# Eight read buffers instead of four, and a new order of the last part, in a fused convolution and feed-forward kernel

## The chip, the cores and the metric

The kernel runs on one core of one Trainium2 chip. The metric is the device time of one execution in microseconds (us). Three timed runs of the kernel before took 190.89, 190.52 and 190.52 us, a median of 190.52.

The engines are named as the profile names them: PE (TensorE, matmuls; PEld its weight loads), DVE (VectorE), ACT (ScalarE), POOL (GpSimd) and SP (SyncE, which here only issues DMAs).

## The reference

The input `x` is [2048, 512] in bfloat16. Two branches work on its normalised rows:

```python
xn = layernorm(x)
kv = causal_conv4(k, shift_k) * v
y  = irfft(rfft(pad(kv)) * rfft(pad(ssm_k)))[:2048] + kv * ssm_D
s  = xn * y
h  = gelu(xn @ w_gate) * (xn @ w_up)      # 512 -> 1792
g  = silu(h @ w_down)                     # 1792 -> 512
return x + s * g
```

So one branch is a long convolution along the 2048 tokens, done through Fourier spectra, and the other is a gated feed-forward block. They meet in the last line.

## The kernel before

Tokens are held 16 to a partition: tile t (0 to 15) is token 16p + t on partition p, 512 channels wide. The transforms are matrix products in two stages, with a trip through DRAM between them (ZH, ZK, ZI), since the second stage needs the data across partitions. The last of these trips is ZI: the inverse transform's first stage (L1027, `inverse`) is copied out of PSUM into the buffers BO, stored to ZI from ACT's DMA queue, and read back into the buffers BI from SP's queue, when all 16 stores have landed. The read number j brings what the pair of tiles 2j and 2j+1 needs.

The feed-forward block works on four groups q of four tiles: 14 units m of gate and up projection (L641), gelu on ACT (L1193), product on DVE into HT (L1202), then the down projection of the group. For groups 0 to 2 the result is made silu by a tanh on ACT (L1234) and one DVE operation (L1236). Group 3 uses ACT's silu itself (L1242), which needs a table load on ACT first.

The last part of the program, from about 150 us on, has these pieces. The short names are used from here on:

- **y0 to y7** (PE, L1277): the second inverse stage of pair j, four matmuls with 64 columns of weights each, two side by side. It reads one BI buffer and fills two PSUM banks.
- **c0 to c7** (ACT or DVE, L1293, recorded in the helper's lines L632, L634, L635): copy of y's PSUM to a BO buffer, 128x1024. For pairs 6 and 7 the copy multiplies by 2.
- **x4, x5** (DVE, L1286): G times XN for pairs 4 and 5; x0 to x3 are done earlier.
- **p0 to p7** (DVE, L1294): product of the copy with G (pairs 0 to 5) or with XN (pairs 6 and 7).
- **a0 to a5** (DVE, L1306): plus X, and **o0 to o5** (SP): the output DMA of the pair, 256 KB.
- **D8 to D11**, **D12 to D15** (PE; L641 for the former, L1223 for the latter): down projection of a tile, in three parts a, b, c of 4, 5 and 5 steps. L1223 does each step in two halves of 64 columns side by side. D15 is 384 columns wide, and its remaining 128 columns, **D15'**, are 14 plain matmuls (L641).
- **s12 to s15, s15'** (ACT, L1242): silu; **m12 to m15'** (DVE, L1244): times the pair's product p6 or p7; **n12 to n15'** (DVE, L1245): plus X; **w12 to w15'** (SP): the output DMA, 128 KB (96 and 32 KB for tile 15).
- **HT0** and so on: the DVE product (L1202) of unit m of group 3.

The order on every engine is written out by hand: `SEQ` (L27 to L50) lists all 816 tasks by number. `Sched.run` (L348) walks that list, gives each task its engine (a trailing `b` takes the second choice, DVE instead of ACT for a copy), takes a free buffer from its pool where it needs one, and the tasks are emitted in that order. Each engine thus works through its own queue in the order of the list; a waiting instruction holds up all behind it on its engine, DMA issues too. Waits are derived from the overlaps of addresses and from use of the same PSUM bank (`Trk._need`, L137). The buffer that a task takes decides which earlier reader it waits for.

The buffers of the last part share room with older ones. HSW (eight slots of four 512-wide rows, 4 KB per partition each) holds the spectra: HS in slots 0 to 3, HW in slots 4 to 7. BI lies at the same address:

```python
HSW = new("HSW", [128, 8, 4, DM], BF16)                  # at kk_at + 2048
BI = at("BI", [128, 4, 4, DM], BF16, kk_at + 2048)
pBI = Pool_("BI", 4)
d_bi = [dsem(f"d_bi{j}") for j in range(4)]
```

Eight reads go through four buffers, so the fifth read takes the buffer of the first and waits until y of that pair has read it. PE is assigned the y tasks in any order that SEQ gives; the reads are issued in an order of their own.

Of the kernel before, what the change touches and what calls it, by code (L numbers as in the profile page):

```python
# [6 lines left out]
BF16 = mybir.dt.bfloat16  # L7
# [7 lines left out]
DM = 512  # L15
# [34 lines left out]
)  # L50
NF_BANKS = 4
ISSUE = 470.0
# [29 lines left out]
class Trk:  # L82
# [29 lines left out]
    def res(self, name, ap):  # L112
        t = ap.tensor
        tn = type(t).__name__
        if tn.startswith("SB"):
            key = "SB"
            addr = self.nc.lookup_mloc(t).addr
        else:
            assert tn.startswith("PS")
            key = "PS:" + t.name  # L120
            addr = 0
        esz = mybir.dt.size(ap.dtype)
        pairs = [list(q) for q in ap.ap]
        pst, pn = pairs[0]
        pstart = ap.offset // pst if pst else 0
        inner = ap.offset - pstart * pst
        hi = sum(st * (n - 1) for st, n in pairs[1:])
        r = Res(name, key, pstart, pstart + pn, addr + inner * esz, addr + (inner + hi + 1) * esz)
        lst = self.res_by_key.setdefault(key, [])
        for o in lst:  # L130
            if o.plo < r.phi and r.plo < o.phi and o.blo < r.bhi and r.blo < o.bhi:
                o.ovl.append(r)
                r.ovl.append(o)
        lst.append(r)
        return r
# [278 lines left out]
def build_kernel(nc, A_q, A_k, A_v, A_shift_k, A_ssm_k, A_ssm_D, B_w_gate, B_w_up, B_w_down, out):  # L414
    with ExitStack() as es0:
# [8 lines left out]
        def at(name, shape, dt, offset):  # L424
            return nc.alloc_sbuf_tensor_at(name, shape, dt, offset=offset)
# [40 lines left out]
        kk_at = place["at"]  # L466
# [27 lines left out]
        BK.append(at("BK2", [128, 4, DM], BF16, skb_at))  # L494
        assert place["at"] <= top, (place["at"], top)
        BO = at("BO", [128, 4, 2, DM], BF16, ast_at)
        BI = at("BI", [128, 4, 4, DM], BF16, kk_at + 2048)
        ast = {"H": [T[:, 4 * j:4 * j + 4, :].rearrange("p (r c) d -> p r c d", c=2) for T in (XN, X) for j in (2, 3)], "K": [AST[:, j, :, :, :] for j in range(2)] + [ASX[:]]}

        ZH = nc.dram_tensor("ZH", [NB * NG, 128, DM], BF16, kind="Internal")  # L500
# [6 lines left out]
        def ps(slot, i=None):  # L507
            if i is None:
                return PSALL[:, 1024 * slot:1024 * (slot + 1)]
            return PSALL[:, 1024 * slot + 512 * i:1024 * slot + 512 * (i + 1)]  # L510
# [7 lines left out]
        res = trk.res  # L518

        def dsem(name):  # L520
            return DSem(nc.alloc_semaphore(name), name)
# [52 lines left out]
                rh[1].ovl.remove(rh[0])  # L574
        R_KB = [res(f"KB{j}", KB[:, j, :, :]) for j in range(6)]
        R_BO = [res(f"BO{j}", BO[:, j, :, :]) for j in range(4)]
        R_BI = [res(f"BI{j}", BI[:, j, :, :]) for j in range(4)]
        R_Z = {"H": [trk.free_res(f"ZH{t}") for t in range(NT // 2)],
               "K": [trk.free_res(f"ZK{t}") for t in range(NT // 2)],
               "I": [trk.free_res(f"ZI{t}") for t in range(16)]}  # L580
# [15 lines left out]
        pHS = Pool_("HS", 4)  # L596
        pHW = Pool_("HW", 4)
        pBO = Pool_("BO", 4)
        pBI = Pool_("BI", 4)

        def pair(T, a, b):

# [10 lines left out]
        def dma(eng, out_ap, in_ap, sem, r, w):  # L613
            trk.dma(eng, lambda e: e.dma_start(out=out_ap, in_=in_ap), sem, r=r, w=w)
# [643 lines left out]
                down(q)  # L1258


        d_bi = [dsem(f"d_bi{j}") for j in range(4)]
        p_y = [B(f"psy{j}", pC) for j in range(8)]
        b_bi = [B(f"bi{j}", pBI) for j in range(8)]
        for j in range(8):
            p, bi = p_y[j], b_bi[j]

            def ld(e, j=j, bi=bi):
                src = bass.AP(ZI, 2 * j * DM, [[16 * DM, 128], [NG * 128 * DM, NB], [DM, 2], [1, DM]])
                dma(e, BI[:, bi.slot, :, :].rearrange("p (b t) d -> p b t d", b=NB), src, d_bi[bi.slot], R_Z["I"], [R_BI[bi.slot]])
            S.add([("SP", ISSUE)], ld, r=bZ["I"], w=[bi], nbytes=W_BI)  # L1270

            def y(e, j=j):
                s, slot = psl(p_y[j]), b_bi[j].slot
                for i in range(2):
                    for b in range(2):
                        c = slice(64 * b, 64 * b + 64)
                        trk.op("PE", lambda h, i=i, b=b, c=c, s=s, slot=slot: h.matmul(ps(s, i)[c, :], lhsT=G1[:, c], rhs=BI[:, slot, 2 * b + i, :], start=True, stop=True, tile_position=(0, 64 * b)),  # L1277
                               r=[R_G1, R_BI[slot]], w=[R_ps[s][i]], accum=True)
            S.add([("PE", 2 * T_FWD)], y, r=[bG1, b_bi[j]], w=[p_y[j]], lat=150.0, mode=3)
# [41 lines left out]
def bass_recurrent_scan__ssm_conv_h3__glu_gated_geglu__prompt_kernel(  # L1321
    nc: bass.Bass,
    A_q: bass.AP,
    A_k: bass.AP,
    A_v: bass.AP,
    A_shift_k: bass.AP,
    A_ssm_k: bass.AP,
    A_ssm_D: bass.AP,
    B_x: bass.AP,
    B_w_gate: bass.AP,  # L1330
    B_w_up: bass.AP,
    B_w_down: bass.AP,
    out: bass.AP,
):
    build_kernel(nc, A_q, A_k, A_v, A_shift_k, A_ssm_k, A_ssm_D, B_w_gate, B_w_up, B_w_down, out)
# [28 lines left out]
```

## Time and profile before

| what | us |
|---|---|
| timed runs, median (lowest to highest) | 190.52 (190.52 to 190.89) |
| the profiled execution, its own time | 191.21 |
| its span, first to last instruction | 189.4 |
| around the span | 1.81 |
| first and last issue of a read into BI | 159.6 and 175.5 |
| first and last issue of an output | 176.2 and 187.4 |
| last matmul ends | 185.5 |
| last DVE operation ends | 187.3 |

The mean granted clock of PE over the span was 0.997. Times in the profile are counted from the start of the span. A row of the timeline gives start, duration, engine, line, operation, output and inputs, shapes and count; in square brackets stands the idle time of the engine before it and what ended it. A line L632, L634, L635, L641 or L614 is that of a helper (copy on ACT, scaled copy on DVE, copy on DVE, matmul, DMA), so the tiles tell which piece it is. A row of the windows gives, for a stretch, its length, the busy time of PE, PEld, DVE, ACT and POOL with counts, the granted clock, the busy share of the DMA engines and GB/s. A row of the DMA issues gives the line, the count, the size, and the median us from issue to landing. A PE row's duration counts the matmuls' modelled ends, so two rows of PE may overlap by some 0.2 us.

### The profile page before, as it was taken

What the parts mean: (1) busy time and instruction counts of PE and PEld (TensorE: products, weight loads), DVE (VectorE), ACT (ScalarE), POOL (GpSimd) and SP (SyncE); (2) the same over time, 40 slices, a digit from 0 to 9 for tenths busy, and PEclk for the clock granted to TensorE, in tenths of its full rate; (3) what the DMA queues carried; (4) which work ended last, traced back from release to release, by engine and by line L of the source; (5) the groups of instructions that cost most, each with busy time, mean ns of one, the idle gap of its engine ahead of it and who ended that gap; (6) DMA issues with size and microseconds to landing.
All of it is one profiled execution on the core that took longest, in us unless ns stands there. A gap on an engine that the chain in (4) does not pass through costs nothing.

```text
span 189.4 us, 3715 instructions
## 1 busy us (share of the span) xinstructions
PE 183.6 (97%) x1474; PEld 82.2 (43%) x1474; DVE 165.6 (87%) x250; ACT 141.5 (75%) x196; POOL 10.4 (5%) x26
## 2 busy tenths in 40 slices
PE   7899999999999999999999999999999999999991
PEld 2685544443333334344444343433343344445551
DVE  7789999999999999978689589998999964657795
ACT  3649796997878799799638897998999575323971
POOL 5211302000000000012000000000000000000000
PEclk9999999999999999999999999999999999999998
DMA  5999999999694986456999997499345254917854
GB/s 180 315 382 288 358 382 360 402 413 233 206 347 154 337 272 223 154 203 230 304 324 165 333 317 246 145 304 320 148 166 170 77 188 141 356 72 265 279 191 154
DMA packets 36422, 47.84 MB, mean 253 GB/s; under 512 B 7347, under 2 KB 26039, under 8 KB 36406
## 3 DMA queue, kind: packets, MB, share of 16 engines
q1 hardware_dynamic: 29878, 39.23, 63.6%
q10 hardware_dynamic: 6528, 8.39, 13.1%
q8 instruction: 11, 0.18, 0.4%
q14 instruction: 5, 0.04, 0.1%
HBM read 27.39 MB, written 14.68 MB: 222 GB/s over the span
## 4 chain that ended last, share of the span: by engine, by line
PE 89%; DVE 4%; DMA 2%; ACT 2%; issue 1%
PE psall L641 73%; PE psall L1027 6%; DMA ZH<-XN 2%; PE psall L1223 2%; PE psall L915 2%; PE psall L949 2%; PE psall L958 2%; PE psall L1277 1%; PE psall L891 1%; DVE G L1294 1%; DVE G L1245 1%; DVE G L1244 1%; DVE G L1306 1%; ACT L1242 1%; ACT XN L632 1%; ACT BO L632 1%
## 5 line engine op out<-in xcount | busy, mean ns | idle before, releaser
L641 PE MATMUL psall<-xnT,Wu 128*128 128x512 bf16 (+1 forms) x248 | 56.0, 359 | 0.0
L641 PE MATMUL psall<-xnT,Wg 128*128 128x512 bf16 (+1 forms) x248 | 55.3, 359 | 0.5 <-DVE xnT L635 0.5
L641 PE MATMUL psall<-Wd,HT 128*128 128x512 bf16 (+1 forms) x182 | 40.6, 367 | 0.0
L1193 ACT ACTIVATE GE<-psall 128x512 bf16<-128x512 f32 x54 | 31.7, 604 | 10.2 <-PE psall L641 9.7
L1202 DVE TENSOR_TENSOR HT<-psall,GE 128x512 bf16<-128x512 f32 x43 | 29.0, 685 | 8.0 <-PE psall L641 7.8
L641 PEld LDWEIGHTS psall<-xnT,Wu 128*128 128x128 bf16 x248 | 22.5, 98 | 25.9 <-issue 2.3
L641 PEld LDWEIGHTS psall<-xnT,Wg 128*128 128x128 bf16 x248 | 21.7, 98 | 26.8 <-issue 2.3
L632 ACT ACTIVATE BO<-psall 128x1024 bf16<-128x1024 f32 x22 | 22.0, 1025 | 9.0 <-PE psall L1277 5.3
L641 PEld LDWEIGHTS psall<-Wd,HT 128*128 128x128 bf16 x182 | 16.1, 98 | 20.9 <-issue 4.1
L1130 DVE TENSOR_TENSOR HSW<-KB,HSW 128x2048 bf16<-128x2048 bf16 x16 | 19.2, 1217 | 0.0
L632 ACT ACTIVATE HSW<-psall 128x1024 bf16<-128x1024 f32 x16 | 15.5, 1034 | 2.3 <-PE psall L1027 2.2
L632 ACT ACTIVATE KB<-psall 128x1024 bf16<-128x1024 f32 x14 | 13.8, 1027 | 2.6 <-PE psall L1027 2.4
L1010 DVE TENSOR_TENSOR KAC<-KAC,KTM 128x2048 bf16<-128x2048 bf16 x12 | 14.6, 1217 | 0.1
L1008 DVE TENSOR_TENSOR KTM<-KK,SKB 128x2048 bf16<-128x2048 bf16 x12 | 14.6, 1215 | 0.1
L632 ACT ACTIVATE AST<-psall 128x1024 bf16<-128x1024 f32 x12 | 12.3, 1023 | 2.3 <-PE psall L949 1.8
L1223 PE MATMUL psall<-Wd,HT 128*64 128x512 bf16 (+1 forms) x112 | 12.0, 366 | 0.0
L1234 ACT ACTIVATE G<-psall 128x512 bf16<-128x512 f32 x12 | 7.2, 596 | 5.7 <-PE psall L641 4.5
L848 DVE BATCH_NORM_STATS2 stats<-X 128x6 f32<-128x512 bf16 x16 | 10.6, 672 | 0.5 <-DMA X<-in_A_q_dram 0.5
L1236 DVE SCALAR_TENSOR_TENSOR G<-G,psall 128x512 bf16<-128x512 bf16 x12 | 8.1, 680 | 3.0 <-ACT G L1234 3.0
L1130 DVE TENSOR_TENSOR KB<-KB,HSW 128x2048 bf16<-128x2048 bf16 x8 | 9.6, 1220 | 0.1
L1153 DVE TENSOR_TENSOR HSW<-HSW 128x2048 bf16<-128x2048 bf16 x8 | 9.5, 1216 | 0.0
L861 POOL TENSOR_TENSOR mv<-mv,NHALF 128x1 f32<-128x1 f32 (+1 forms) x7 | 5.3, 757 | 71.0 <-DVE mv L859 66.3
(90 smaller groups left out, 178.5 us busy)
## 6 DMA issues: line engine op xcount, KB each, us to landing
BH<-ZH SPq DMA_DIRECT2D x8, 512.0 KB, 5.4
BK<-ZK SPq DMA_DIRECT2D x8, 512.0 KB, 5.8
HSW<-HSW SPq DMA_DIRECT2D x16, 256.0 KB, 3.2
ZI<-BO ACTq DMA_DIRECT2D x16, 256.0 KB, 2.6
BI<-ZI SPq DMA_DIRECT2D x8, 512.0 KB, 4.9
ZK<-AST SPq DMA_DIRECT2D x6, 512.0 KB, 3.3
Hn<-in_A_ssm_k_dram SPq DMA_DIRECT2D x4, 512.0 KB, 7.6
KK<-in_A_k_dram SPq DMA_DIRECT2D x4, 512.0 KB, 10.9
```

The costliest lines, as they stand in the source:

```text
L632: return h.activation(o, i, ACTF.Copy, scale=scale)
L641: return h.matmul(o, lhsT=l, rhs=r, start=st, stop=sp)
L848: t_stats[t] = op([("DVE", 670.0)], lambda e, h, t=t: h.bn_stats(stats[:, t, :], X[:, t, :]), r=[bX[q][t % 4]], w=[bst[t]], rr=[R_X[t]], w ...
L1008: op([("DVE", dur)], lambda e, h, j=j, m=m: h.tensor_tensor(KTM[:, m.slot, :, :], kk(j), sk(j), ALU.mult), r=need + [bSKB[j], a], w=[m], r ...
L1010: op([("DVE", dur)], lambda e, h, m=m: h.tensor_tensor(KAC[:, a.slot, :, :], KAC[:, a.slot, :, :], KTM[:, m.slot, :, :], ALU.add), r=[m], ...
L1027: trk.op("PE", lambda h: h.matmul(ps(s, i)[b, :], lhsT=wt(col)[a, :], rhs=data(col)[a, :], start=n < 16, stop=n >= len(todo) - 16, tile_po ...
L1130: return hd.tensor_tensor(pair(KB, *(2 * DM * z for z in slots())) if to else x, k, x, ALU.mult)
L1153: return hd.tensor_tensor(x, x, y, ALU.add)
L1193: op([("ACT", act(512))], lambda e, h: h.activation(GE[:, g.slot, :], bank(pg), ACTF.Gelu_apprx_tanh), r=[pg], w=[g], rr=lambda: R_bank(pg ...
L1202: op([("DVE", dve(512, 1))], lambda e, h: h.tensor_tensor(HT[:, q % 2, m, :], bank(pu), GE[:, g.slot, :], ALU.mult), r=[pu, g], w=[bHT[q][m]],
L1223: trk.op("PE", lambda h, m=m, i=i, c=c: h.matmul(pc()[c, :], lhsT=HT[:, q % 2, m, 128 * jt + 64 * i:128 * jt + 64 * i + 64], rhs=Wd[:, m, ...
L1236: op([("DVE", dve(512, 1))], lambda e, h, g=g, pc=pc: h.scalar_tensor_tensor(out=g, in0=g, scalar=1.0, in1=pc(), op0=ALU.add, op1=ALU.mult ...
```

## The change

BI grows to eight buffers, so that it covers all of HSW, with a pool of eight and eight semaphores. The last five lines of SEQ are replaced: from task 350 on, some 150 tasks stand in another order, and two copies change their engine.

```diff
-        BI = at("BI", [128, 4, 4, DM], BF16, kk_at + 2048)
+        BI = at("BI", [128, 8, 4, DM], BF16, kk_at + 2048)
-        R_BI = [res(f"BI{j}", BI[:, j, :, :]) for j in range(4)]
+        R_BI = [res(f"BI{j}", BI[:, j, :, :]) for j in range(8)]
-        pBI = Pool_("BI", 4)
+        pBI = Pool_("BI", 8)
-        d_bi = [dsem(f"d_bi{j}") for j in range(4)]
+        d_bi = [dsem(f"d_bi{j}") for j in range(8)]
```

```diff
-    "639 353 634 654 640 342 310 325 354 343 344 346 345 355 334 337 338 335 336 641 655 347 323 348 356 357 358 359 656 657 350 351 644 645 646 647 349 "
-    "360 361 363b 364 649 362 642 650 651 652 643 731 703 705 653 658 711 712 713 714 745 675 677 676 704 762 706 723 678 715 725 648 708 710 717 716 718 "
-    "683 724 726 684 732 685 686 748 749 746 767 768 733 734 759 776 751b 752 806 783 784 785 739 740 760 804 741 742 763 790 761 812 786 787 777 778 737 "
-    "738 788 764 814 735 779 743 736 754 755 757 808 769 770 744 765 807 805 758 810 815 813 771 772 809 766 773 789 811 780 791 792 793 797 798 799 800 "
-    "774 781 775 782 794 795 796 801 802 803 "
+    "639 353 634 654 640 342 310 325 354 343 344 346 345 355 334 337 338 335 336 641 655 347 323 348 356 357 350 649 358 642 359 656 657 351 650 651 643 "
+    "360 363b 644 645 646 349 361 362 364 723 725 724 726 708 731 745 652 653 658 647 683 685 711 703 648 710 704 712 705 715 706 675 713 714 677 684 676 "
+    "717 716 732 762 733 737 748 678 746 686 718 734 769 767b 790 783 738 749 751 804 757 768 741 784 735 742 785 752 758 763 743 786 806 759 776 736 764 "
+    "777 787 810 744 754 814 755 778 739 765 815 740 770 771 788 808 805 779 791 766 809 760 780 772 781 792 761 797 812 773 789 811 782 793 798 807 774 "
+    "794 799 800 795 801 813 802 775 796 803 "
```

Put into the short names, engine by engine (psi3 and psi7 are the last two first stages of the inverse; g and u a unit's gate and up projection; t and r the tanh L1234 and the operation L1236 of a tile):

| engine | before | after |
|---|---|---|
| PE, to the units' end | psi3, D11c, D9abc, psi7, D10abc, g7 g9 u9 g0 u0 u7 g12 g10 u8 u10 g2 u12 u2 | psi3, D10a, D11c, D10bc, psi7, D9abc, g12 u12 u8 g2 g9 g7 u7 u9 g10 g0 u2 u0 u10 |
| PE, from there | y0 y7 y1, D13a, D14abc, y4 y5, D15a, D13bc, y3 y2, D12ab, y6, D12c, D15bc, D15' | y0 y7 y1, D12a, D15a, D14a, y3, D14b, y5, D14c, D13a, y2, D13b, y6, D13c, y4, D12bc, D15bc, D15' |
| ACT, from y0 | c0 c7 c4 c5, table load, s14 s13 c2 c3 c6 s12 s15 s15' | c0 c1 c3 c5, table load, s14 c2 c6 s13 c4 s12 s15 s15' |
| DVE, from the last HT | p0 p7 x4 c1 p1 a1 a0 p4 a4 m14 n14 p5 a5 p2 a2 p3 a3 p6 m12 m13 n12 n13 m15 n15 m15' n15' | c7 p0 a0 p7 p1 p3 a1 x4 p5 m14 a3 a5 p2 n14 a2 p6 m13 n13 p4 a4 m12 n12 m15 n15 m15' n15' |
| SP, reads of ZI for pair | 0 7 1 4 5 3 2 6 | 0 7 1 3 5 2 6 4 |
| SP, outputs | o1 o0 o5 o4 o2 w14 o3 w12 w13 w15 w15' | o5 o0 o2 w14 o3 w13 o1 o4 w12 w15 w15' |

Before the last HT, DVE's queue changes with the units: the last three products are HT0, HT2, HT10 (before HT10, HT12, HT2), and r8 stands before the copy of psi7 instead of behind it. On ACT the second copy of psi3 comes before the tanh of tiles 8 and 11 instead of after one of them, and the tanh of tiles 10 and 9 comes behind the gelu of unit 12. Copy c1 goes from DVE to ACT and c7 from ACT to DVE. No task is added or left out, and everything up to task 357 stands as it was.

## The prediction

> **What bounds the kernel now.** I read the page first, for the load of each engine, and then the chain of work that ended last, cut to its final 70 us.
>
> ```profile
> PE 183.6 (97%) x1474; PEld 82.2 (43%) x1474; DVE 165.6 (87%) x250; ACT 141.5 (75%) x196; POOL 10.4 (5%) x26
> ```
>
> ```profile
> 155.31 14.35 PE psall L641 x66
> 169.66 1.42 PE psall L1277 x12
> 171.08 3.88 PE psall L1223 x36
> 174.96 0.86 PE psall L1277 x8
> ...
> 176.38 1.02 ACT BO L632
> ...
> 177.42 1.28 ACT L1242
> 178.71 0.61 ACT G L1242
> ...
> 179.34 0.44 DVE G L1244
> ...
> 187.11 0.23 DVE G L1245
> ```
>
> Up to 176 us the chain is TensorE without a hole: 66 matmuls in 14.35 us, then y0, y7, y1 (L1277), then the last down projection (L1223). After that it leaves TensorE for a copy on ACT, the table load of the first silu, and then DVE to the end. So two stages with two limits: TensorE's queue, and behind it a tail on ACT and DVE. The timeline of the last 5 us shows how far the tail trails:
>
> ```profile
> 184.51 0.95 PE L641 MATMUL psall<-Wd,HT 128*128 128x128 bf16 x14
> 184.64 0.49 ACT L1242 ACTIVATE G<-psall 128x384 bf16<-128x384 f32 x1 [1.03 <-PE psall L1223]
> 184.85 0.76 DVE L1244 TENSOR_TENSOR G<-G,XN 128x512 bf16<-128x512 bf16 x2
> 185.50 0.28 ACT L1242 ACTIVATE G<-psall 128x128 bf16<-128x128 f32 x1 [0.37 <-PE psall L641]
> 185.53 0.75 DVE L1245 TENSOR_TENSOR G<-G,X 128x512 bf16<-128x512 bf16 x2
> ...
> 186.86 0.22 DVE L1244 TENSOR_TENSOR G<-G,XN 128x128 bf16<-128x128 bf16 x1
> 187.11 0.23 DVE L1245 TENSOR_TENSOR G<-G,X 128x128 bf16<-128x128 bf16 x1
> ```
>
> TensorE ends at 184.51 + 0.95 = 185.46, the last silu at 185.78, DVE at 187.34. With an empty queue DVE would need only m15' and n15' behind that silu: 185.81 + 0.22 + 0.03 + 0.23 = 186.29. DVE's backlog therefore costs 187.34 - 186.29 = 1.05 us. That is all the tail can give back while TensorE stays gapless.
>
> Where the backlog comes from:
>
> ```profile
> 175.46 1.94 ACT L632 ACTIVATE BO<-psall 128x1024 bf16<-128x1024 f32 x2 [3.24 <-PE psall L1277]
> ...
> 177.42 1.28 ACT L1242 ACT_TABLE_LOAD   x1
> 178.71 1.08 ACT L1242 ACTIVATE G<-psall 128x512 bf16<-128x512 f32 x2
> ...
> 179.34 0.42 DVE L1244 TENSOR_TENSOR G<-G,XN 128x512 bf16<-128x512 bf16 x1 [1.27 <-ACT G L1242]
> ...
> 180.15 0.68 DVE L1294 TENSOR_TENSOR G<-BO,G 128x1024 bf16<-128x1024 bf16 x1
> 180.86 0.69 DVE L1306 TENSOR_TENSOR G<-G,X 128x1024 bf16<-128x1024 bf16 x1
> 181.47 0.68 DVE L1294 TENSOR_TENSOR G<-BO,G 128x1024 bf16<-128x1024 bf16 x1
> ```
>
> c4 and c5 came late (ACT idle 3.24 us for y4), the table load stood behind them, and DVE stood 1.27 us before m14. From 179.34 it never stopped again. The last three rows give DVE's pace: an independent successor of a wide product or sum starts 0.61 after its predecessor's start (180.86 to 181.47), one that needs the predecessor's result 0.71 after it (180.15 to 180.86).
>
> **The change, part by part.**
>
> *Eight buffers.* The reads of ZI now all go out at once instead of four waiting for L1277.
>
> ```profile
> L1277 PEld LDWEIGHTS psall<-BI,G 128*64 128x64 bf16 x32 | 1.7, 110 | 1.9 <-DVE HT L1202 0.4
> BI<-ZI SPq DMA_DIRECT2D x8, 512.0 KB, 4.9
> 159.62 0.37 SPq L614 DMA_DIRECT2D BI<-ZI  x1
> 162.00:164.00 2.00, 2.00 (x11) 0.93 (x10) 0.77 (x2) 0.53 (x1) 0.00 (x0) 1.00 1.05 363
> ```
>
> L1277 waited for no read (its one wait, 0.4, is on DVE), so the buffers by themselves are worth 0. What they allow is the order. Eight reads are 4.19 MB; at the 363 GB/s of 162 to 164 us they take 11.6 us, so with the first issue at 159.6 the last lands near 173. The latest need is y4 near 180.4; the tightest is y1, third in both orders. Slots 4 to 7 overwrite spectra last read before 155.4, so no wait is added there. Cost 0; if a read came 7 us late, TensorE would stand.
>
> *TensorE.* Same matmuls and the same number of changes of tile shape. I checked the banks that each group now takes. One wait moves forward: D10's first part stands right behind psi3 and needs the bank that ACT's copy of psi6 frees.
>
> ```profile
> 149.26 1.02 ACT L632 ACTIVATE BO<-psall 128x1024 bf16<-128x1024 f32 x1 [0.44 <-ACT BO L632]
> 150.46 4.28 PE L641 MATMUL psall<-Wd,HT 128*128 128x512 bf16 x19
> 168.84 0.69 DVE L1202 TENSOR_TENSOR HT<-psall,GE 128x512 bf16<-128x512 f32 x1 [1.03 <-PE psall L641]
> 173.47 1.22 DVE L635 CAST BO<-psall 128x1024 bf16<-128x1024 f32 x1
> ```
>
> The copy ends at 150.28, TensorE arrives at 150.46: 0.18 to spare, cost 0. If it were late, everything behind it in TensorE's queue would move by that. The other tight places: y7 needs HT0 (169.53) at 170.15, y1 needs HT2 (170.13) at 170.6, y4 needs c2 (179.32) at 180.36. So TensorE again ends at 185.46. From the chain's rows, four L1277 take 0.43 and a 512-wide L1223 0.108 each (0.081 at 384), so in the new order the ends are: y7 170.65, y1 171.08, y3 173.89, y5 175.40, D14 176.48, y2 177.77, y6 179.28, D13 180.36, y4 180.79, D12 182.95, D15 184.58.
>
> *ACT* (start 0.07 behind TensorE, copies 0.92 apart, in the new order): c0 170.28 to 171.30, c1 to 172.22, c3 to 174.98, c5 175.47 to 176.49, table load to 177.79, s14 to 178.40, c2 to 179.32, c6 179.35 to 180.37, s13 181.03, c4 181.95, s12 183.62, s15 185.13, s15' 185.78. The load stands ahead of s14's wait, as before.
>
> *DVE.* c7 moves here as a multiplication by 2 from PSUM (L634), a form the trace lacks at this size. The nearest is the CAST above, 1.22; ACT's copies take 1.02, and two 512-wide PSUM operations of 0.69 would be 1.38. I take 1.22; either end vanishes in the wait before p3. Starts: HT0 168.84 (the row above, same place in TensorE's queue), HT2 169.44, HT10 170.04, c7 170.72, p0 171.86, a0 172.58, p7 173.19, p1 173.80, p3 175.01 (waits 0.6 for c3), a1 175.62, x4 176.23, p5 176.84, m14 178.43 (waits 1.0 for s14), a3 178.77, a5 179.38, p2 179.99, n14 180.60, a2 180.94, p6 181.55, m13 182.27, n13 182.72, p4 183.06, a4 183.78, m12 184.39, n12 184.84, m15 185.18, n15 185.56, m15' 185.86, n15' 186.11. End 186.34.
>
> So DVE ends 187.34 - 186.34 = **1.00 us earlier**. Of it, idle between HT and the end falls from 0.88 + 0.22 + 1.27 = 2.37 to 1.6 (0.8), about three fewer neighbours that need each other's result give 0.3; the later end of HT (170.74 for 170.46) takes part of it back.
>
> *Output.* SP's queue is new: o5 is first, and o0, o2, w14, o3, w13, o1, o4 stand behind waits.
>
> ```profile
> 176.16 11.63 SPq L614 DMA_DIRECT2D out_dram<-G  x11
> 185.97 1.82 SPq L614 DMA_DIRECT2D out_dram<-G  x4
> out_dram<-G SPq DMA_DIRECT2D x6, 256.0 KB, 2.2
> out_dram<-G SPq DMA_DIRECT2D x1, 32.0 KB, 1.6
> 176.00:178.00 2.00, 2.00 (x22) 1.12 (x20) 1.96 (x4) 1.98 (x3) 0.00 (x0) 1.00 0.69 179
> 182.00:184.00 2.00, 2.00 (x26) 1.25 (x24) 1.93 (x4) 1.56 (x2) 0.00 (x0) 1.00 0.81 300
> 184.00:186.00 2.00, 1.46 (x22) 0.93 (x18) 1.97 (x6) 0.77 (x2) 0.00 (x0) 1.00 0.80 290
> ```
>
> Nothing leaves before a5 ends at 180.07 (before: 176.16). From o2 at 181.70 on, 1.57 MB remain. In 182 to 186 the queues moved 300 / 0.81 and 290 / 0.80, about 365 GB/s when busy: 4.3 us from 182.5 (0.8 after an issue) to 186.8. w15' is issued at 186.4 and its data would start at 187.2, so it finds the engines free, barely. It lands 1.6 later, as before, and the end moves with DVE. The Trainium skill ("DMA: Bandwidth & Descriptors", Rules for kernel authors) says to issue a DMA early and wait late, which speaks against this queue; by that rule the held outputs are a loss, and the slower rival below gives its price. Its 341 GB/s for a 1 MB load would, as an estimate, put the end of the data at 187.1, still ahead of w15'.
>
> **Sum.** TensorE 0, ACT 0, DVE -1.00, output 0. The profiled execution took 191.21 us, 189.4 of it span and 1.81 around it; it would become 190.2. The three timed runs lie below it, median 190.52 (to 190.89). I take the same 1.0 off that median: **189.5 us**.
>
> **Rivals.**
>
> *The tail is not so well packed:* the sum over 29 DVE operations has no slack behind p5, and every late arrival is kept. If half the backlog stays, the time is 190.0. For it: m15 starts 0.05 behind its silu by my count. Against it: every row used repeats within 0.01.
>
> *It does nothing:* reads never bound, and something else holds the end. 190.5. Against it: 1.05 us of backlog stand plainly between the last silu and the last sum.
>
> *Slower, the output drains late:* most of the output now has to pass between 180.1 and 187, and at a low rate w15' stands in line. The end meets that of before when the data ends 1.0 later than w15' would on an idle queue, at about 188.3: 1.57 MB in 5.8 us, 271 GB/s. At the 179 GB/s of 176 to 178 us it would take 8.8 us and the time would be near 193.5; at 250 GB/s, 191.0. For it: that row. Against it: those two microseconds mixed reads of ZI with outputs, and now the reads are over by 173; with outputs alone it was 365.
>
> *Slower, the table load drains ACT:* if 1.38 us more lay between the load and s14, m14 and all of DVE behind it would move by 1.38: 190.9. By the rows the load began 0.02 after the copy and the silu 0.01 after the load, so the chance is small. The 1.38 is the drain that the Trainium skill ("ScalarE: Activation LUTs", What ACT_TABLE_LOAD costs) adds to a load; this trace has its 1283 ns and no drain.
>
> **How the numbers follow.** Forecast 0.73 and half the gain 0.09: faster. No effect 0.07: same. Late output 0.09 and table drain 0.02: slower. Faster 0.82, same 0.07, slower 0.11; under 0.2% (0.38 us) nothing can be told. The range runs from 189.1 (the bound of 1.05 and the 0.3 by which timed runs differ) to 190.4 (half the gain and the same 0.4).
>
> **What would show it.** Right: TensorE still ends within 0.1 of 185.46 with no wait in front of D10 or any L1277; the load begins near 176.5; DVE waits about 0.6 before p3 and 1.0 before m14; m15' follows the last silu at once; DVE ends near 186.3; w15' lands in 1.6. Wrong: a hole in TensorE's queue between 150 and 171, DVE still in arrears at 185.8, or w15' landing in over 2.5 us.

## The result, and the profile after

The changed kernel takes 189.46 us (median; 188.99 to 190.74) against 190.51 us (190.03 to 191.69): a ratio of 0.9942, with a 95% interval of 0.9928 to 0.9957, about 1.1 us less. Its profiled execution took 189.08 us, 187.3 of them span.

The chain of work that ended last, in the changed kernel (start, duration, what):

```profile
154.24 14.35 PE psall L641 x66
168.59 1.42 PE psall L1277 x12
...
174.32 1.94 PE psall L1223 x18
176.26 0.48 PE psall L1277 x4
176.74 0.59 ACT G L1242
...
177.36 0.43 DVE G L1244
...
185.01 0.22 DVE G L1245
```

It has the same two stages: 66 matmuls in 14.35 us without a hole, then the last down projection, then the first silu and DVE. The copy is gone from it, and so, as drawn, is the table load. Here the view needs care: it leads from y2's end to the silu, but y2 is no input of s14, and the load ends at 175.43 + 1.28 = 176.71, just as y2 does. The silu still waits for the load: in e7 below, with the load out of the way, it starts 6.95 us behind y0 (175.80 - 168.85) and here 8.21 us (176.73 - 168.52). The timeline of the end, to be laid beside that of before:

```profile
183.43 0.96 PE L641 MATMUL psall<-Wd,HT 128*128 128x128 bf16 x14
183.57 0.49 ACT L1242 ACTIVATE G<-psall 128x384 bf16<-128x384 f32 x1 [1.03 <-PE psall L1223]
...
184.09 0.36 DVE L1244 TENSOR_TENSOR G<-G,XN 128x384 bf16<-128x384 bf16 x1
184.43 0.28 ACT L1242 ACTIVATE G<-psall 128x128 bf16<-128x128 f32 x1 [0.37 <-PE psall L641]
184.49 0.36 DVE L1245 TENSOR_TENSOR G<-G,X 128x384 bf16<-128x384 bf16 x1
184.76 0.22 DVE L1244 TENSOR_TENSOR G<-G,XN 128x128 bf16<-128x128 bf16 x1
185.01 0.22 DVE L1245 TENSOR_TENSOR G<-G,X 128x128 bf16<-128x128 bf16 x1
```

TensorE ends at 183.43 + 0.96 = 184.39 and DVE at 185.23: a lag of 0.84 us, where it was 187.34 - 185.46 = 1.88. m15' starts at 184.76, 0.05 behind the end of its silu (184.71); before, it started 1.08 behind. The lag fell by 1.04 us, which is the gain.

The span fell by 2.1 us, twice as much, and that has to be taken apart before anything is read from it. TensorE before, then after, in its first 9 us:

```profile
1.21 5.30 PE L641 MATMUL psall<-AST 128*128 128x512 bf16 x12 [1.21 <-DVE Q L726]
...
8.76 0.45 PE L641 MATMUL psall<-xnT,Wg 128*128 128x128 bf16 x5 [0.52 <-DVE xnT L635]
```

```profile
1.21 4.37 PE L641 MATMUL psall<-AST 128*128 128x512 bf16 x12 [1.21 <-DVE Q L726]
...
7.83 1.07 PE L641 MATMUL psall<-xnT,Wg 128*128 128x128 bf16 x16 [0.66 <-DVE xnT L635]
```

The first 12 matmuls took 5.30 us in one execution and 4.37 in the other, in code that is the same, and the first gate matmul starts 0.93 us apart (8.76 and 7.83). y0 starts at 169.59 before and at 168.52 after, 1.07 apart. The order is not the reason: in e1, with the old order, y0 starts at 168.37, and in e0, the changed kernel once more, at 169.10. From y0 to TensorE's end it is 15.87 us in both. So times of the two profiles are compared below after a shift of 1.07 us, and the medians, over 22 runs each, show only the other half.

With that shift the rows show where the 1.04 us come from. c5 (174.39 + 1.07 = 175.46) starts just when c4 did, but it alone stands ahead of the table load, where c4 and c5 stood. The load starts at 176.50 instead of 177.42, 0.92 earlier, which is the pace of one copy, and m14 at 178.43 instead of 179.34, 0.91 earlier. Behind m14 DVE has as many operations as before, seven wide and nine small ones, and takes 7.87 us from m14's start to its end, where it took 8.00. So 0.91 of the gain is the earlier load, and 0.13 is a denser queue behind it.

### The profile page after: what moved, and what is told of

Read it like the earlier page. It is cut to its first block, busy times and chain, and to the rows that moved or that the text cites. A ratio compares the mean times of both kernels' runs of the same rounds, so it can differ in the third digit from the quotient of the medians.

```text
span 187.3 us, 3717 instructions
## 1 busy us (share of the span) xinstructions
PE 182.4 (97%) x1474; PEld 81.5 (44%) x1474; DVE 164.9 (88%) x250; ACT 141.1 (75%) x196; POOL 10.9 (6%) x26
## 4 chain that ended last, share of the span: by engine, by line
PE 90%; DVE 4%; DMA 3%; issue 0%; SPq 0%; ACT 0%
PE psall L641 73%; PE psall L1027 6%; PE psall L1223 3%; DMA X<-in_A_q_dram 3%; PE psall L949 2%; PE psall L958 2%; PE psall L915 2%; PE psall L1277 1%; DVE G L1306 1%; DVE G L1245 1%; DVE G L1244 1%; PE psall L891 1%; DVE G L1294 1%; SPq L614 0%; DVE XN L1294 0%
## 5 line engine op out<-in xcount | busy, mean ns | idle before, releaser
L1234 ACT ACTIVATE G<-psall 128x512 bf16<-128x512 f32 x12 | 6.9, 599 | 3.2 <-PE psall L641 3.2
L1236 DVE SCALAR_TENSOR_TENSOR G<-G,psall 128x512 bf16<-128x512 bf16 x12 | 8.0, 681 | 1.2 <-ACT G L1234 1.2
```

The source lines that it names most:

```text
L1236: op([("DVE", dve(512, 1))], lambda e, h, g=g, pc=pc: h.scalar_tensor_tensor(out=g, in0=g, scalar=1.0, in1=pc(), op0=ALU.add, op1=ALU.mult ...
```

## The experiments

| kernel | ratio to before (95% interval) | lag of DVE's end behind TensorE's, us |
|---|---|---|
| changed kernel | 0.9942 (0.9928 to 0.9957) | 0.84 |
| changed kernel once more (e0) | 0.9934 (0.9916 to 0.9952) | 0.86 |
| e1: old order, eight buffers | 0.9988 (0.9973 to 1.0003) | 1.87 |
| e2: new order, four buffers | 0.9946 (0.9926 to 0.9966) | 0.86 |
| e3: old order, one silu moved | 0.9948 (0.9930 to 0.9967) | 1.03 |
| e4: new order, outputs early | 0.9935 (0.9913 to 0.9957) | 0.85 |
| e5: new order, extra DVE work before p3 | 0.9938 (0.9920 to 0.9957) | 0.86 |
| e6: new order, extra DVE work behind m14 | 0.9970 (0.9958 to 0.9982) | 1.44 |
| e7: new order, table load early | 0.9944 (0.9926 to 0.9961) | 0.86 |

The lags are from one profile each, worked out as above: before, 1.88.

The theory was that the order makes the gain by clearing DVE's backlog, and that the buffers are worth nothing by themselves. The first rival: the reads that go out early are what helps. e1 and e2 take the two halves of the change apart.

**e1**, the kernel before with the four lines of BI as changed (two are shown) and SEQ as it was:

```diff
-        BI = at("BI", [128, 4, 4, DM], BF16, kk_at + 2048)
+        BI = at("BI", [128, 8, 4, DM], BF16, kk_at + 2048)
...
-        pBI = Pool_("BI", 4)
+        pBI = Pool_("BI", 8)
```

> The old order with eight buffers. If the order alone makes the gain: the reads go out in one burst, but no matmul of L1277 waited for a read before, so the tail is as before (DVE ends 1.9 us behind TensorE) and the ratio to the kernel before is 1.000 within 0.002. If earlier reads are what helps: most of the 0.6% is there, a ratio of 0.995.

The ratio is 0.9988 and its interval holds 1. Its view of the tile BI, and then its timeline:

```profile
L614 SPq DMA_DIRECT2D BI<-ZI x8: 365/472/625, 158.7 to 162.3; - x8
```

```profile
178.12 0.43 DVE L1244 TENSOR_TENSOR G<-G,XN 128x512 bf16<-128x512 bf16 x1 [1.27 <-ACT G L1242]
183.29 0.96 PE L641 MATMUL psall<-Wd,HT 128*128 128x128 bf16 x14
...
185.90 0.22 DVE L1245 TENSOR_TENSOR G<-G,X 128x128 bf16<-128x128 bf16 x1
```

All eight reads are issued by 162.3, 13 us earlier than before, and the tail stays as it was: DVE waits the same 1.27 before m14. Earlier reads alone do nothing that can be measured: the lag is 1.87 beside 1.88.

**e2**, the changed kernel with those four lines put back to four buffers (one is shown):

```diff
-        pBI = Pool_("BI", 8)
+        pBI = Pool_("BI", 4)
```

> The new order with four buffers. The reads 5 to 8 (pairs 5, 2, 6, 4) wait for y0, y7, y1 and y3, and by the profile of the changed kernel would land near 172.7, 174.5, 176 and 177, each about 1 us or more ahead of its L1277 (173.7, 176.1, 177.6, 179.1), and ahead of the first output at 179.0. If the buffers are worth nothing even here: ratio 0.994, as the changed kernel. If the new order needs them: a hole in TensorE's queue in front of y5 or y4, and a ratio of 0.997 or more; with 1 us of hole, 1.000.

The gain is there: 0.9946, lag 0.86. What was missed is small: one read was late. TensorE's weight loads in e2, and the same place in the changed kernel:

```profile
177.10 0.33 PEld L1223 LDWEIGHTS psall<-Wd,HT 128*64 128x64 bf16 x4
177.82 0.14 PEld L1277 LDWEIGHTS psall<-BI,G 128*64 128x64 bf16 x4 [0.39 <-DMA BI<-ZI]
```

```profile
176.96 0.33 PEld L1223 LDWEIGHTS psall<-Wd,HT 128*64 128x64 bf16 x4
177.40 0.33 PEld L1277 LDWEIGHTS psall<-BI,G 128*64 128x64 bf16 x4
```

y6 waited until 177.82 for its read, which was expected near 176; it was the third of those that went out together behind y0, y7 and y1 (its landing took 7.5 us, the longest in e2). The hole shows in TensorE's own length: from y0's start (168.65) to the end (184.62) 15.97 us instead of 15.87; in the nine other profiles it is 15.86 to 15.88. So in the new order the eight buffers are worth 0.1 us, one part in ten of the gain, by this one profile; the timed runs cannot tell it from nothing.

**e3** asks where in the order the gain lies. One task of the old order is moved: s14, and with it the table load, ahead of c4 and c5.

```diff
-    ... 785 739 740 760 804 741 742 763 790 761 812 786 787 ...
+    ... 785 786 739 740 760 804 741 742 763 790 761 812 787 ...
```

> The old order and four buffers, with one task moved: the silu of tile 14, and with it the table load, stands ahead of the copies c4 and c5 on ACT, where ACT sat idle for 3.24 us. If the backlog of DVE came from the load standing between c5 and the silu: the load is hidden, m14 starts near 178.0 instead of 179.3, DVE ends near 186.47 instead of 187.34, ratio 0.9955. If the whole new order is needed: 0.999 to 1.000.

The timeline of e3:

```profile
171.73 1.28 ACT L1242 ACT_TABLE_LOAD   x1
...
174.52 0.60 ACT L1242 ACTIVATE G<-psall 128x512 bf16<-128x512 f32 x1 [1.51 <-PE psall L1223]
...
177.47 0.42 DVE L1244 TENSOR_TENSOR G<-G,XN 128x512 bf16<-128x512 bf16 x1
...
180.11 0.69 DVE L1294 TENSOR_TENSOR G<-BO,G 128x1024 bf16<-128x1024 bf16 x1 [0.44 <-ACT BO L632]
...
184.00 0.96 PE L641 MATMUL psall<-Wd,HT 128*128 128x128 bf16 x14
...
185.76 0.23 DVE L1245 TENSOR_TENSOR G<-G,X 128x128 bf16<-128x128 bf16 x1
```

The load falls into idle time: ACT waits 1.51 us for D14 behind it anyway. m14 starts with no wait, and the lag is 1.03. Of the wait of 1.27 us that is gone, 0.44 comes back in front of p2, which waits for its copy c2. One moved silu so gives 1.88 - 1.03 = 0.85 of the 1.04 us. In time e3 and the changed kernel cannot be told apart (0.9948 and 0.9942). The backlog came from the place of the load and its silu, which moved together here; the load alone was not moved in the old order. The rest of the new order (132 of the 816 entries of SEQ come behind the first difference) adds about 0.2 us in the profile.

**e4** tests the rival of the output: o0, o1 and o3 (tasks 805, 807, 811) stand ahead of o5 (815).

```diff
-    ... 739 765 815 740 ... 808 805 779 ... 809 ... 811 ... 807 ...
+    ... 739 765 805 807 811 815 740 ... 808 779 ... 809 ...
```

> The changed kernel with the outputs o0, o1 and o3 put ahead of o5 in SP's queue, so that the first leaves when its sum is done, near 172 instead of 179. If DVE's end sets the time: ratio 0.994, as the changed kernel, within 0.001. If the burst of outputs between 179 and 186 holds the end: 0.992 or less.

The windows of e4, then of the changed kernel (last two columns: busy share of the DMA engines, GB/s):

```profile
180.00:182.00 2.00, 2.00 (x22) 1.06 (x20) 1.97 (x5) 1.33 (x2) 0.00 (x0) 1.00 0.63 234
182.00:184.00 2.00, 2.00 (x26) 1.20 (x23) 1.93 (x5) 0.60 (x1) 0.00 (x0) 1.00 0.67 236
184.00:186.00 2.00, 0.85 (x14) 0.68 (x13) 1.60 (x6) 0.77 (x2) 0.00 (x0) 1.00 0.55 197
```

```profile
180.00:182.00 2.00, 2.00 (x22) 1.12 (x20) 1.93 (x5) 0.92 (x2) 0.00 (x0) 1.00 0.94 349
182.00:184.00 2.00, 2.00 (x30) 1.36 (x25) 1.93 (x5) 0.97 (x2) 0.00 (x0) 1.00 1.04 368
184.00:186.00 2.00, 0.39 (x7) 0.21 (x4) 1.17 (x5) 0.34 (x2) 0.00 (x0) 1.00 0.81 287
```

The last output in the changed kernel's DMA issues (us to landing):

```profile
out_dram<-G SPq DMA_DIRECT2D x1, 32.0 KB, 1.5
```

In the changed kernel the DMA engines are full from 180 to 184 (0.94 and 1.04), in e4 half to two thirds so from 180 to 186 (0.63, 0.67, 0.55), and the time is the same (0.9935, beside 0.9942 and 0.9934). The last output lands in 1.5 us either way. The Trainium skill's rule to issue a DMA early ("DMA: Bandwidth & Descriptors", Rules for kernel authors) is not borne out as a gain here: in the changed kernel the DMA engines fall idle (0 GB/s near 186.1) just before the data of the last output moves.

**e5 and e6** put the same extra product of DVE (128x1024, 0.61 us of its queue, on buffers no longer used) at two places: in front of p3, inside a wait, and behind m14.

```diff
+        op([("DVE", dve(1024, 2))], lambda e, h: h.tensor_tensor(KB[:, 0, :, :], KB[:, 1, :, :], KB[:, 2, :, :], ALU.mult), rr=R_KB[1:3], ww=R_KB[0:1])
...
-    ... 735 742 785 752 758 ...
+    ... 735 742 785 752 816 758 ...
```

That is e5; e6 has the same added task, and in SEQ

```diff
-    ... 736 764 777 787 810 ...
+    ... 736 764 777 787 816 810 ...
```

> The changed kernel with one more DVE product (128x1024, of buffers that are no longer used) in front of p3, where DVE waits 0.54 us for c3. If DVE's queue has slack only in its waits: 0.07 of the 0.61 us reaches p3, the wait before m14 (0.92) takes the rest, and the time is that of the changed kernel within 0.1 us. If DVE's load as a whole sets the time: 0.6 us later.

> The same extra product behind m14, behind the last wait. If nothing behind m14 has slack: DVE ends 0.6 us later, the ratio to the kernel before is 0.9975. If TensorE's end alone sets the time and DVE follows: no change, 0.994.

DVE in e5:

```profile
173.15 0.68 DVE L1310 TENSOR_TENSOR KB<-KB 128x1024 bf16<-128x1024 bf16 x1
173.78 0.69 DVE L1294 TENSOR_TENSOR G<-BO,G 128x1024 bf16<-128x1024 bf16 x1
...
177.19 0.43 DVE L1244 TENSOR_TENSOR G<-G,XN 128x512 bf16<-128x512 bf16 x1 [0.92 <-ACT G L1242]
```

DVE in e6:

```profile
178.04 0.68 DVE L1310 TENSOR_TENSOR KB<-KB 128x1024 bf16<-128x1024 bf16 x1
...
185.95 0.23 DVE L1245 TENSOR_TENSOR G<-G,X 128x128 bf16<-128x128 bf16 x1
```

In e5 the product is swallowed: the wait before m14 is the same 0.92, the lag 0.86, the ratio 0.9938. In e6 it goes through to the end: lag 1.44, 0.58 more, and the ratio 0.9970 lies above that of e5 with no overlap of the intervals. This shows the cause itself: behind its last wait DVE's queue sets the time, nearly one for one (0.58 of 0.61 us), and ahead of that wait the same 0.61 us, which fit into the waits of 0.54 and 0.92, cost nothing.

**e7** asks whether there is more to get. The table load is pulled into ACT's idle time by a silu of one column behind the last gelu.

```diff
+        op([("ACT", act(1))], lambda e, h: h.activation(COLS[:, 1:2], COLS[:, 0:1], ACTF.Silu), rr=[R_cols], ww=[R_col1])
...
-    ... 717 716 ...
+    ... 717 816 716 ...
```

> The changed kernel with a silu of one column (128x1) right behind the last gelu on ACT, so that the table load falls into ACT's idle time near 168 us and the silu of tile 14 follows its matmuls. DVE's wait of 0.92 before m14 goes. If the tail already stands at the floor that the last silu sets (m15' starts 0.05 behind it): no gain, ratio 0.994 within 0.001. If the load still holds DVE back: 0.9 us more, 0.9895.

ACT and DVE in e7:

```profile
167.47 1.28 ACT L1310 ACT_TABLE_LOAD   x1
...
175.80 0.60 ACT L1242 ACTIVATE G<-psall 128x512 bf16<-128x512 f32 x1
```

```profile
176.68 0.42 DVE L1244 TENSOR_TENSOR G<-G,XN 128x512 bf16<-128x512 bf16 x1
...
182.91 0.43 DVE L1244 TENSOR_TENSOR G<-G,XN 128x512 bf16<-128x512 bf16 x1 [0.21 <-ACT G L1242]
...
184.43 0.36 DVE L1244 TENSOR_TENSOR G<-G,XN 128x384 bf16<-128x384 bf16 x1 [0.63 <-ACT G L1242]
```

The wait before m14 is gone and comes back as waits of 0.21 and 0.63 before m12 and m15; lag 0.86, ratio 0.9944. The tail stands at its floor, which is TensorE's end and one short silu, product and sum. No experiment here beats the changed kernel; what is left to shorten is TensorE's own queue.

## Why the prediction was right

Forecast 189.5, measured 189.46. To hit it within 0.04 us is luck: the interval of the ratio alone is 0.0029 wide, 0.55 us. But the steps hold one by one, so the mechanism is not luck. The rows of the changed kernel on which this rests, besides those above:

```profile
149.38 3.78 PEld L641 LDWEIGHTS psall<-Wd,HT 128*128 128x128 bf16 x19 [0.39 <-ACT BO L632]
...
168.52 1.49 PE L1277 MATMUL psall<-BI,G 128*64 128x512 bf16 x12
...
173.94 0.69 DVE L1294 TENSOR_TENSOR G<-BO,G 128x1024 bf16<-128x1024 bf16 x1 [0.54 <-ACT BO L632]
...
175.43 1.28 ACT L1242 ACT_TABLE_LOAD   x1
176.73 0.60 ACT L1242 ACTIVATE G<-psall 128x512 bf16<-128x512 f32 x1
177.36 0.43 DVE L1244 TENSOR_TENSOR G<-G,XN 128x512 bf16<-128x512 bf16 x1 [0.92 <-ACT G L1242]
```

- *TensorE 0:* 15.87 us from y0 to the end in both, the same 14.35 us for the 66 matmuls ahead of it. The bank for D10's first part was in time: the copy of psi6 ends at 149.20 and D10 starts at 149.38, the 0.18 to spare that were predicted, and the idle time in front of its weight loads is the 0.39 of before, though the profile now puts it down to the copy. The 0.4 us in front of the first L1277, which the profile of before puts down to DVE and the prediction called its one wait, stands in the changed kernel too, put down to issue; it did not end with the DVE product.
- *ACT:* the load starts at 175.43 + 1.07 = 176.50 (predicted near 176.5). The silu follows it by 0.02.
- *DVE -1.00:* p3 at 175.01 and m14 at 178.43 after the shift, both as predicted to the hundredth; the end at 186.30 against 186.34 predicted; waits 0.54 and 0.92 where 0.6 and 1.0 were said. Half the backlog, the first rival, would have left a lag near 1.4, and no effect one of 1.88; it is 0.84. c7 as a multiplication from PSUM took 1.22 (169.64 to 170.86 in the timeline), as the cast.
- *Buffers 0:* shown by e1. All reads had landed by 172.2, 173.3 after the shift, where near 173 was predicted. That they are worth 0.1 in the new order (e2) the prediction did not say.
- *Output 0:* 349 and 368 GB/s with outputs alone, where 365 was assumed, and the last output lands in 1.5 us, where 1.6 was; e4 shows that the burst costs nothing.
- *Table drain:* load and silu are 0.02 apart here and in e7 the load and the small silu 0.01 (167.47 + 1.28 = 168.75, then 168.76). The further 1.38 us of the Trainium skill ("ScalarE: Activation LUTs", What ACT_TABLE_LOAD costs) appear in none of these runs.

Some things the text had too simple. It split DVE's 1.00 us over the whole queue from the last HT on: 0.8 less idle time and 0.3 from fewer dependent neighbours, less 0.28 for the later HT. These pieces make only 0.82; the 1.00 stands on the list of starts. By the rows they are 0.91, 0.39 and 0.26, which make the measured 1.04. More important, a split that starts ahead of the wait before m14 does not name the cause: what stands there costs nothing (e5), and 0.91 us come from the earlier load, which one moved silu gives nearly as well (0.85 in e3). And the text expected 190.2 for the profiled execution, which took 189.08: the profiles differ by another microsecond that is no effect of the change. The forecast itself rested on the median and was not touched by that. The range counts the spread of the three timed runs, 0.37 us, once as 0.3 and once as 0.4.

## What to carry to other kernels

Where a matmul queue runs to the end without a hole, measure the lag from its last matmul to the last operation of the engines behind it, and subtract what an empty queue would need: that difference, 1.05 us here, is the most that reordering the tail can give, and 1.04 were got. Then look for the last wait in front of the backlog: here work ahead of it was free as far as it fitted into the wait (e5), and work behind it cost one for one (e6). A table load is a task with a place of its own: try it where its engine waits anyway, before buying buffers or moving everything else.

## What the runs showed of the hardware that was not expected

Executions of the same instructions differ in the first 9 us. In the ten profiles here, whose code is the same up to 149 us, y0 starts between 168.36 and 169.59 us. Between the profiles of before and after, 0.93 of the 1.07 us is there by the first gate matmul (8.76 and 7.83 us), with 5.30 and 4.37 us for the first 12 matmuls. The weight loads show how: at first they step by 0.42 to 0.43 us per matmul in every profile, later by about 0.21. The change comes between 4.1 and 5.0 us in eight profiles, but in the kernel before and in e4 not by 5.9, when the weights of all 12 are loaded. That is not all of it: in e0 the 12 matmuls took 4.29 us, and the first gate matmul still came at 8.69, with a wait of 0.60 us for a read of the input `ssm_k` on the way. The granted clock shows nothing: it reads 1.00 in 0 to 4 and in 4 to 8 us of both kernels. Why the pace changes sooner in one execution than in another was not tried and stays open. The difference is as large as the effect under study, so single spans would have told nothing.
